# Two more features of one token block by Strassen's seven products, in a fused attention and two-MLP kernel

## The chip, the cores and the metric

The kernel runs on one core of a Trainium2 chip. The metric is the device time of one execution in microseconds (us); before the change it is 573.19 us, the median of three runs (573.0 to 573.52).

## The reference

Attention with 4 sink keys and a window of 128 (2 batches, 8 heads, 768 positions, head size 64) gives 1536 tokens of 512 values. Two MLPs follow, each with 2048 hidden values:

```
keep = is_sink | in_window
a = softmax(where(keep, q @ k.T / 8, -1e9));  x = a @ v        # (1536, 512)
h = x @ w1_in;  g = h * clip(h + 3, 0, 6) / 6;  x = g @ w1_out  # first MLP
h = x @ w2_in;  g = h * sigmoid(1.702 * h);     y = g @ w2_out  # second MLP
```

All inputs, weights included, are given in 64 bits; the kernel converts the weights on the chip. The output is in 32-bit floats.

## The kernel before

The 1536 tokens are three blocks of 512, named by their first token: 0, 512 and 1024. The 2048 hidden values are 16 features of 128. Every operand of a matmul is split into a high and a low part, and every product is made of three matmuls (high x high, high x low, low x high). An ordinary item is one feature of one block: `up` makes four products of 512 columns (12 matmuls, L1143) and a gate, `down` makes four (12 matmuls, L1192).

The first MLP's items are, in this order: block 0 features 0 to 7, block 512 features 0 to 7 and 8 to 15, block 1024 features 0 to 7 (the list `BLOCKS`), then features 8 to 15 of blocks 0 and 1024 together (items of kind "both" and "rest", for the blocks named by `BOTH`). Item 24 is the first of block 1024, items 30 and 31 are its features 6 and 7, item 32 is the first "both".

Both features of a "both" pair are made by Strassen's scheme. The up-projection of two features for the 512 tokens is seen as a product of 2 x 2 blocks, which takes seven block products in place of eight. `weights` combines the weights of the two features (four additions or subtractions of 256 columns on DVE, L610) and splits four operands (casts at L450 and L452, subtractions at L563). `half_pair` makes the seven products, each of 6 matmuls of 256 columns (L723), and puts them together: `put` copies (L740), `add` adds (L747), `clip` makes the gate in two steps (L756, L761). Ordinary items have their gate at L1155 and L1160. The sums of the tokens that Strassen's scheme needs are made by `halve`, once for a block: for each of four slices a copy on the SP queue (L812) and an adding DMA on the POOL queue (L817) into a buffer of the ring "spare", then subtractions (L826), casts (L836) and subtractions for the low parts (L841). Its operand t1 takes the place of half of the block's own columns in `xy`. In the kernel before, `halve` is called for both blocks at the first "both" item.

The order of the work on each engine is found ahead of time by a planner (`Plan.issue`): it puts each operation on an engine and takes, among those that could start within SLACK of the soonest, the one with the earliest due time. Operations that two engines can do go to the one with the smaller end, where PACT and PDVE make ACT and DVE look slower by that share. Due times come from constants: attention tiles from RAMP0, RAMP, PAIR and PAIR2, items from RAMP0, RAMP, START and the rates RATE (the first 8 items) and RATE2 (the next 16), their down-projections DOWN later. A long operation waits up to HOLD for one that is due MARGIN sooner. On the chip each engine runs its own list in that order and waits only for its operands and buffers.

Attention (12 tiles of 128 tokens; scores L1366, transposes L1417, values L1440 and L1448, softmax L1381, L1389, L1398, L1408) and weight conversion (L480, L485, L493, L501, L508 for each feature of each MLP) are mixed with the first MLP's items. The second MLP takes block 512 by ordinary items and blocks 0 and 1024 together by another Strassen scheme (L635, L939). Per MLP product, the names in the rows are: `w0h`, `w0l` the split input weights, `wg` the ring that holds the split output weights and the gates, `sh`, `sl` split combinations, `xt` the split token sums.

Of the kernel before, what the change touches and what calls it, by code (L numbers as in the profile page):

```python
# [33 lines left out]
NVB = 3  # L34
NVC = 3
SLACK = 50
HOLD = 425
MARGIN = 18538
LONG = 1000
ISSUE = 1300  # L40
ADD_DMA = 4500
PACT = 0.1
PDVE = 0.5
STRETCH = 1.0
LATER = 1000000
H_BANKS = 3
RAMP0 = 7993
RAMP = 1510
PAIR = 4538
PAIR2 = 5889  # L50
DOWN = 7000
START = 3000
RATE = 1.61
RATE2 = 1.21
NU = 3
NG = 2
PX = 8
# [3 lines left out]

BLOCKS = [(0, 0, 8), (512, 0, 8), (512, 8, 16), (1024, 0, 8)]
BOTH = (0, 1024)

# [5 lines left out]
def tile_sink_window_attention_moe_moe2(  # L72
# [164 lines left out]
    with tc.tile_pool(name="msk", bufs=1) as mp:  # L237
# [6 lines left out]
        t0 = mp.tile([P, P], F32, name="t0")  # L244
# [270 lines left out]
    def plan_mlps(plan, blocks, item_due, late=None):  # L515
# [27 lines left out]
        def split(i, part):  # L543
            f = items[i][3]
            return split_of(plan.wf[f], slice(512 * part, 512 * (part + 1)), f"w{part}", part, i >= second - NF + 4)
# [24 lines left out]
        def split_g(u, after, act=True):  # L570
            gh, gl = Buf(cls="gh"), Buf(cls="gl")
            plan.op(
                [("ACT", 520)] + ([] if act else [("DVE", 335)]),
                lambda e: copy(e, gh.tile, parted(u.tile)), after, reads=[u], writes=[gh], chain="g",
            )
            plan.op(
                [("DVE", 602)],
                lambda e: e.tensor_tensor(  # L578
                    out=gl.tile, in0=parted(u.tile), in1=gh.tile.bitcast(F32), op=ALU.subtract
                ),  # L580
                after, reads=[u, gh], writes=[gl],
            )
            return gh, gl
# [9 lines left out]
        def weights(i, cls):  # L593

            f1, f2 = items[i][3], items[i][3] + 1
            w1, w2 = plan.wf[f1], plan.wf[f2]
            a11, a12 = (lambda x=x: w1.tile.bitcast(F32)[:, x * 256 : (x + 1) * 256] for x in range(2))
            a21, a22 = (lambda x=x: w2.tile.bitcast(F32)[:, x * 256 : (x + 1) * 256] for x in range(2))
            sa, sb = Buf(cls=cls, kind="m"), Buf(cls=cls, kind="m")
            s1, s4 = (lambda x=x: sa.tile[:, x * 256 : (x + 1) * 256] for x in range(2))  # L600
            s3, s2 = (lambda x=x: sb.tile[:, x * 256 : (x + 1) * 256] for x in range(2))
            for to, x, y, how, reads, into in (
                (s1, a21, a22, ALU.add, [w2], sa),
                (s3, a11, a21, ALU.subtract, [w1, w2], sb),
                (s2, s1, a11, ALU.subtract, [w1, sa], sb),
                (s4, a12, s2, ALU.subtract, [w1, sb], sa),
            ):
                plan.op(
                    [("DVE", 335)],
                    lambda e, to=to, x=x, y=y, how=how: e.tensor_tensor(out=to(), in0=x(), in1=y(), op=how),  # L610
                    None, reads=reads, writes=[into], chain="mix",
                )
            full = slice(0, 512)
            wa, wb = split_of(w1, full, "w0"), split_of(sb, full, "s")
            wc, wd = split_of(sa, full, "w0"), split_of(w2, slice(256, 512), "s")
            return wa, wb, wc, wd
# [62 lines left out]
        def both(i):  # L679

            if i in g:
                return
            if i == second:
                for t0 in BOTH:
                    halve(t0, due[i])
            ws = weights(i, "spare")
            us = half_pair(i, BOTH[0], ws, [Buf(cls="u") for _ in range(2)], due[i])
            for n, u in enumerate(us):
                g[i + n] = split_g(u, due[i] + 6000, False)
            holes = []  # L690
            for n in range(2):
                w = plan.wf[items[i + n][3]]
                holes.append(Buf(wf[items[i + n][3]].bitcast(F32)[:, :512]))
                holes[n].readers = list(w.readers)
            half_pair(i, BOTH[1], ws, holes, due[i] + 7 * 672)
            for n in range(2):
                wo[i + n] = split(i + n, 1)
                kept_u[items[i + n][3]] = holes[n]

        def rest_of(i):  # L700

# [101 lines left out]
        def halve(t0, when):  # L803

            s, first, last = t0 // 512, slice(0, P), slice(P, 256)
            extra[t0, "t1"] = True
            full = [Buf(cls="spare") for _ in range(NC)]
            x = [[b for half in halves(t0, 512) for b in plan.x[half][c]] for c in range(NC)]
            for c in range(NC):
                plan.op(  # L810
                    [("SP", 262144 / RATE_DMA)],
                    lambda e, c=c: e.dma_start(out=parted(full[c].tile), in_=xyl[s][:, :, c, :].bitcast(F32)),  # L812
                    when, reads=x[c], writes=[full[c]], after=plan.done,
                )
                plan.op(
                    [("POOL", ADD_DMA)],
                    lambda e, c=c: e.dma_start(  # L817
                        out=parted(full[c].tile), in_=xyh[s][:, :, c, :].bitcast(F32), accum_op=ALU.add
                    ),
                    when, reads=x[c], writes=[full[c]],  # L820
                )

            def take(a, ac, b, bc, to, tc):
                plan.op(
                    [("DVE", 335)],
                    lambda e: e.tensor_tensor(  # L826
                        out=parted(to.tile)[:, :, tc], in0=parted(a.tile)[:, :, ac], in1=parted(b.tile)[:, :, bc],
                        op=ALU.subtract,
                    ),
                    when, reads=[y for y in (a, b) if y is not to], writes=[to],  # L830
                )

            def parts(src, cols, hi, lo, his, los):
                n = cols.stop - cols.start
                plan.op(
                    [("ACT", 520 if n > P else 300)], lambda e: e.copy(hi(), parted(src.tile)[:, :, cols]), when,  # L836
                    reads=[src], writes=his,
                )
                plan.op(
                    [("DVE", 602 if n > P else 335)],  # L840
                    lambda e: e.tensor_tensor(  # L841
                        out=lo(), in0=parted(src.tile)[:, :, cols], in1=hi().bitcast(F32), op=ALU.subtract
                    ),
                    when, reads=[src] + his, writes=los,
                )

            for j in range(2):
                a, b = full[j], full[2 + j]
                for t in ("t2", "t3", "t4"):
                    extra[t0, t, j] = [Buf(), Buf()]  # L850
                e0 = 6 * BOTH.index(t0) + 3 * j
                at = lambda k, cols, e0=e0: late()["x"](e0 + k)[:, :, cols]
                take(a, last, a, first, a, first)
                take(b, last, a, last, a, last)
                take(b, last, a, first, b, last)
                take(b, first, b, last, b, first)
                both = extra[t0, "t2", j]
                extra[t0, "t4", j] = both
                parts(b, slice(0, 256), lambda at=at: at(0, slice(0, 256)), lambda at=at: at(1, slice(0, 256)), both[:1], both[1:])
                hi, lo = extra[t0, "t3", j]  # L860
                parts(a, last, lambda at=at: at(2, first), lambda at=at: at(2, last), [hi], [lo])
                his, los = ([plan.x[half][j][k] for half in halves(t0, 512)] for k in range(2))
                parts(
                    a, first, lambda j=j: xyh[s][:, :, j, last], lambda j=j: xyl[s][:, :, j, last], his, los,
                )
# [387 lines left out]
        for i in range(len(items)):  # L1253
            f = items[i][3]
            if first_use.get(f) == i:
                plan_convert(plan, f, None)
                if f + nst < NF:
                    plan_load_w(plan, w1, f + nst, None)
                else:
                    plan_load_w(plan, w2, f + nst - NF, None)  # L1260
            {"pair": pair, "both": both, "rest": rest_of}.get(items[i][0], up)(i)
            if i:
                down(i - 1)
            f = items[i][3]
            if i < second + NF and last_use[f] == i:
                plan_convert(plan, f, None)
                if f + nst < NF:
                    plan_load_w(plan, w2, f + nst, None)
# [453 lines left out]
```

## Time and profile before

| | before |
|---|---|
| median of the runs | 573.19 us |
| the profiled execution | 572.57 us |
| its span | 570.8 us |
| PE busy | 555.3 us (97%) |
| DVE busy | 483.1 us (85%) |
| ACT busy | 398.0 us (70%) |
| POOL busy | 64.0 us (11%) |
| chain that ended last, by engine | PE 90%, DVE 4%, DMA 2%, issue 1%, SP queue 1% |

PE is the matmul engine, PEld its weight loads, DVE the vector engine, ACT the scalar engine, POOL and SP the two that issue DMAs here. The chain is followed back from the last instruction: at each step to what released it, or to the instruction before it on its engine.

### The profile page before, as it was taken

How to read it: one execution, taken by the hardware profiler on the slowest of the kernel's cores; microseconds unless marked ns; L12 is line 12 of the kernel's file. 1: busy time of each engine (PE TensorE's matmuls, PEld its weight loads, DVE VectorE, ACT ScalarE, POOL GpSimd, SP SyncE). 2: the span in 40 equal slices, each digit the busy share in tenths (PEclk: the TensorE clock that was granted, in tenths of full speed). 3: DMA queues.
4: the chain of work that ended last, by engine and by line, in shares of the span. 5: the costliest groups of instructions: out<-in, count | busy, mean ns of one | idle time of the engine just before them, and what ended most of it. 6: DMA issues, size and time to landing. Idle time of an engine off the chain costs nothing.

```text
span 570.8 us, 11900 instructions
## 1 busy us (share of the span) xinstructions
PE 555.3 (97%) x4626; PEld 496.0 (87%) x4626; DVE 483.1 (85%) x1045; ACT 398.0 (70%) x849; POOL 64.0 (11%) x70
## 2 busy tenths in 40 slices
PE   6799999999999999999999999999999999999996
PEld 6678888888888888889999888888888888999996
DVE  6899999989999579999999999999567655667784
ACT  6798888854747587577775575765479787768762
POOL 0000000000000212000000000000013334765000
PEclk9989999999999999999999999999999999999998
DMA  8985544143352724212224043223034477999512
GB/s 260 373 253 189 170 145 162 42 140 126 114 170 82 179 79 71 45 66 75 75 75 144 5 148 130 91 88 134 0 93 75 75 108 149 169 183 198 98 38 79
DMA packets 27824, 69.89 MB, mean 122 GB/s; under 512 B 2736, under 2 KB 15024, under 8 KB 23664
## 3 DMA queue, kind: packets, MB, share of 16 engines
q1 hardware_dynamic: 15248, 53.06, 28.0%
q0 software_dynamic: 12224, 15.73, 17.5%
q8 instruction: 38, 0.62, 0.5%
q10 hardware_dynamic: 288, 0.26, 0.2%
q14 instruction: 26, 0.21, 0.1%
HBM read 47.02 MB, written 3.15 MB: 88 GB/s over the span
## 4 chain that ended last, share of the span: by engine, by line
PE 90%; DVE 4%; DMA 2%; issue 1%; SPq 1%; ACT 0%
PE bank L1192 29%; PE bank L1143 21%; PE bank L939 13%; PE bank L635 13%; PE bank L723 7%; PE bank L1417 3%; PE bank L1366 2%; DMA wf<-in_kq_dram 2%; PE bank L1440 1%; PE bank L1448 1%; DVE wf L501 1%; DVE pexp L1381 1%; DVE wf L508 1%; DVE pexp L1408 0%; DVE wf L493 0%
## 5 line engine op out<-in xcount | busy, mean ns | idle before, releaser
L1192 PE MATMUL bank<-wg 128*128 128x512 f32 x768 | 188.5, 381 | 0.3 <-DVE u L1160 0.3
L1192 PEld LDWEIGHTS bank<-wg 128*128 128x128 f32 x768 | 142.0, 189 | 19.6 <-DVE u L1160 0.7
L1143 PE MATMUL bank<-xy,w0h 128*128 128x512 f32 x384 | 116.4, 384 | 1.4 <-ACT xy L450 1.1
L1143 PEld LDWEIGHTS bank<-xy,w0h 128*128 128x128 f32 x384 | 71.1, 189 | 11.9 <-issue 1.3
L450 ACT CAST wg<-wf 128x512 fp32r<-128x512 f32 x83 | 51.1, 618 | 33.6 <-PE bank L1192 24.8
L1143 PE MATMUL bank<-xy,w0l 128*128 128x512 f32 x192 | 72.9, 380 | 0.1
L887 POOL DMA_DIRECT2D wf<-wf x24 | 29.0, 1301 | 228.5 <-ACT wf L868 193.1
L1389 ACT ACTIVATE pexp<-pexp,nb 128x196 f32<-128x196 f32 x96 | 43.1, 452 | 9.1 <-DVE nb L1381 8.9
L563 DVE TENSOR_TENSOR wg<-wf,wg 128x512 fp32r<-128x512 f32 x64 | 44.1, 690 | 5.8 <-ACT wg L450 5.6
L563 DVE TENSOR_TENSOR w0l<-wf,w0h 128x512 fp32r<-128x512 f32 x60 | 41.2, 687 | 3.6 <-ACT w0h L450 3.4
L480 ACT ACTIVATE wf<-stage 128x1024 f32<-128x1024 f32 x32 | 37.8, 1183 | 7.9 <-DMA stage<-in_w_dram 7.9
L1143 PEld LDWEIGHTS bank<-xy,w0l 128*128 128x128 f32 x192 | 36.3, 189 | 5.6 <-DVE w0l L563 0.5
L1155 ACT ACTIVATE u<-bank,three 128x512 f32<-128x512 f32 x32 | 21.8, 681 | 25.4 <-PE bank L1143 25.4
L578 DVE TENSOR_TENSOR wg<-u,wg 128x512 fp32r<-128x512 f32 x56 | 38.3, 689 | 1.3 <-ACT wg L450 1.0
L501 DVE SCALAR_TENSOR_TENSOR wf<-stage,wf 128x1024 int32<-128x1024 int32 x32 | 39.1, 1223 | 0.1
L508 DVE SCALAR_TENSOR_TENSOR wf<-stage,wf 128x1024 int32<-128x1024 int32 x32 | 39.1, 1221 | 0.0
L589 ACT ACTIVATE u<-bank 128x512 f32<-128x512 f32 x32 | 19.1, 596 | 27.4 <-PE bank L1143 20.0
L635 PE MATMUL bank<-xy,w0h 128*128 128x512 f32 x128 | 38.1, 379 | 0.0
L450 ACT CAST wg<-u 128x512 fp32r<-128x512 f32 x47 | 29.0, 621 | 6.8 <-DVE u L1160 4.4
L1381 DVE CUSTOM_DVE_ANT_0 pexp<-bank,mask 128x196 f32<-128x196 f32 x96 | 30.6, 356 | 1.3 <-ACT pexp L1389 0.4
L1417 PE MATMUL bank<-ident,pexp 128*128 128x128 f32 x192 | 28.8, 294 | 2.8 <-DVE pexp L1408 2.6
L1417 PEld LDWEIGHTS bank<-ident,pexp 128*128 128x128 f32 x192 | 24.0, 151 | 6.8 <-issue 2.5
(245 smaller groups left out, 1220.2 us busy)
## 6 DMA issues: line engine op xcount, KB each, us to landing
stage<-in_w_dram SPq DMA_DIRECT2D x32, 1024.0 KB, 4.9
wf<-wf POOLq DMA_DIRECT2D x24, 256.0 KB, 3.8
wf<-in_kq_dram SPq DMA_DIRECT2D x8, 520.0 KB, 11.2
vc<-in_vc_dram SPq DMA_DIRECT2D x12, 320.0 KB, 4.9
vb<-in_v_dram SPq DMA_DIRECT2D x10, 256.0 KB, 6.2
kept<-in_kq_dram SPq DMA_DIRECT2D x4, 520.0 KB, 11.2
vc<-xy SPq DMA_DIRECT2D x7, 256.0 KB, 2.6
vc<-xy POOLq DMA_DIRECT2D x7, 256.0 KB, 4.7
```

Source lines behind the costliest of these rows:

```text
L450: eng.copy(out, in_)
L501: lambda e: e.scalar_tensor_tensor(out=w.tile, in0=top, scalar=-0x40000000, in1=w.tile, op0=ALU.bitwise_and, op1=ALU.bitwise_or),
L508: lambda e: e.scalar_tensor_tensor(out=w.tile, in0=low, scalar=29, in1=w.tile, op0=ALU.logical_shift_right, op1=ALU.bitwise_or),
L563: lambda e: e.tensor_tensor(out=lo.tile[at], in0=of(), in1=hi.tile[at].bitcast(F32), op=ALU.subtract),
L578: lambda e: e.tensor_tensor(out=gl.tile, in0=parted(u.tile), in1=gh.tile.bitcast(F32), op=ALU.subtract),
L635: e.matmul(bank.tile, l, woven(r), start=(begin and j == 0 and k == 0), stop=(j == 1 and k == 2), skip_group_check=True,)
L723: e.matmul(bank.tile[:, :256], l, woven(r), start=(begin and j == 0 and k == 0), stop=(j == 1 and k == 2), skip_group_check=True,)
L939: e.matmul(to, l, woven(t), start=(begin and n == 0 and m == 0 and e4 % share == 0), stop=(n == pairs - 1 and m == 2), skip_group_check=True,)
L1143: e.matmul(h.tile[:, :n], w, woven(x), start=(c == 0 and k == 0), stop=(c == NC - 1 and k == 2))
L1192: e.matmul(yb.tile, l, woven(r), start=(begin and k == 0), stop=(end is not None and k == 2))
L1389: lambda e, n=n: e.activation(pes[n].tile[:, :W], pes[n].tile[:, :W], AF.Exp, bias=nbs[n].tile, scale=-1.0, accum_out=z.tile[:, n : n + 1],),
L1417: e.transpose(pt.tile[:, n * P : (n + 1) * P], pes[2 * a + j].tile[:, x * P : (x + 1) * P], ident)
```

## The change

A constant OWN = 6 is added. The items of block 1024 with feature 6 or more (features 6 and 7, items 30 and 31) are made by a new function `own`: it calls `halve` for block 1024 if that is not done, combines the weights of the pair and calls `half_pair` for block 1024 alone. `both` calls `halve` for each block that has none yet, so for block 0 only. Nine planner constants are changed as well.

```diff
-HOLD = 425
+HOLD = 376
-PDVE = 0.5
+PDVE = 0.71
-RAMP0 = 7993
+RAMP0 = 7638
-PAIR = 4538
-PAIR2 = 5889
-DOWN = 7000
-START = 3000
+PAIR = 4370
+PAIR2 = 5073
+DOWN = 6456
+START = 344
-RATE2 = 1.21
+RATE2 = 1.1
+OWN = 6
...
-            if i == second:
-                for t0 in BOTH:
+            for t0 in BOTH:
+                if (t0, "t1") not in extra:
                     halve(t0, due[i])
...
+        def own(i):
+
+            if i in g:
+                return
+            if (BOTH[1], "t1") not in extra:
+                halve(BOTH[1], due[i])
+            ws = weights(i, "spare")
+            for n, u in enumerate(half_pair(i, BOTH[1], ws, [Buf(cls="u") for _ in range(2)], due[i])):
+                g[i + n] = split_g(u, due[i] + 6000, False)
+                wo[i + n] = split(i + n, 1)
...
-            {"pair": pair, "both": both, "rest": rest_of}.get(items[i][0], up)(i)
+            alone = late and items[i][0] == 1 and items[i][1] == BOTH[1] and items[i][3] >= OWN
+            {"pair": pair, "both": both, "rest": rest_of, 1: own if alone else up}.get(items[i][0], up)(i)
```

## Rows read from the trace of the kernel before

**Rows 1.** Busy time by stretch: stretch, length, each engine's busy us (instructions), clock, DMA.
```profile
20.00:40.00 20.00, 16.45 (x410) 14.11 (x410) 17.27 (x64) 16.95 (x54) 0.00 (x0) 0.91 0.98 335
40.00:60.00 20.00, 18.17 (x230) 15.31 (x226) 19.93 (x54) 16.72 (x42) 0.00 (x0) 1.00 0.60 183
60.00:560.00 500.00, 500.00 (x3614) 447.71 (x3612) 426.79 (x835) 349.65 (x705) 62.58 (x60) 1.00 0.42 106
```

**Rows 2.** Chain of waits, whole span: start us, length us, what.
```profile
5.44 12.08 DMA wf<-in_kq_dram
...
24.32 2.92 issue
...
58.54 4.80 PE bank L1192 x21
...
490.60 75.05 PE bank L939 x672
```

**Rows 3.** Chain of waits from 32.6 to 58.5 us, shares by line.
```profile
by line: DVE wf L501 13.1%; DVE pexp L1381 12.5%; DVE wf L508 12.1%; DVE pexp L1408 8.4%; DVE wf L493 7.1%; DVE wf L485 7.0%; DVE u L1160 7.0%; issue 5.2%; DVE wg L578 5.0%; DVE w0l L563 4.8%; DVE xy L1467 4.7%; DVE wg L563 4.7%; DVE z L139
```

**Rows 4.** Chain of waits, runs of matmuls of 512 (L1192) and 256 columns (L723).
```profile
329.33 7.77 PE bank L1192 x36
...
265.77 2.68 PE bank L723 x24
...
257.52 4.98 PE bank L723 x42
```

**Rows 5.** Groups by line and shape: count | busy us, mean ns | idle before, releaser.
```profile
L563 DVE TENSOR_TENSOR w0l<-wf,w0h 128x512 fp32r<-128x512 f32 x60 | 41.2, 687 | 3.6 <-ACT w0h L450 3.4
...
L723 PEld LDWEIGHTS bank<-xy,w0h 128*128 128x128 f32 x128 | 20.3, 191 | 0.9 <-ACT vb L740 0.2
...
L1160 DVE SCALAR_TENSOR_TENSOR u<-u,bank 128x512 f32<-128x512 f32 x32 | 21.8, 683 | 6.7 <-ACT u L1155 6.6
...
L610 DVE TENSOR_TENSOR aside<-wf 128x256 f32<-128x256 f32 x16 | 6.7, 422 | 0.0
...
L756 ACT ACTIVATE u<-bank,three 128x256 f32<-128x256 f32 x12 | 5.4, 473 | 2.9 <-PE bank L723 1.6 <-DVE bank L747 1.4
...
L761 DVE SCALAR_TENSOR_TENSOR u<-u,bank 128x256 f32<-128x256 f32 x12 | 4.8, 418 | 0.5 <-ACT u L756 0.4
```

**Rows 6.** Busy time by stretch, from 180 to 400 us.
```profile
180.00:220.00 40.00, 40.00 (x357) 34.52 (x356) 29.66 (x66) 27.33 (x58) 8.77 (x7) 1.00 0.54 119
220.00:400.00 180.00, 180.00 (x995) 162.04 (x994) 177.02 (x310) 117.77 (x220) 1.22 (x1) 1.00 0.25 86
```

**Rows 7.** Timeline near 400 us: start us, length us, instruction, idle before.
```profile
400.44 1.24 DVE L508 SCALAR_TENSOR_TENSOR wf<-stage,wf 128x1024 int32<-128x1024 int32 x1
...
403.67 0.69 DVE L563 TENSOR_TENSOR w0l<-wf,w0h 128x512 fp32r<-128x512 f32 x1 [1.38 <-ACT w0h L450]
...
408.16 0.59 PE L1143 MATMUL bank<-xy,w0h 128*128 128x512 f32 x2
```

**Rows 8.** DMA issues of `halve`: count, KB each, us from issue to landing.
```profile
vc<-xy SPq DMA_DIRECT2D x7, 256.0 KB, 2.6
vc<-xy POOLq DMA_DIRECT2D x7, 256.0 KB, 4.7
```

**Rows 9.** Groups by line and shape, the adding DMAs of `halve`.
```profile
L817 POOL DMA_DIRECT2D vc<-xy x7 | 9.1, 1528 | 29.3 <-PE bank L1192 16.0 <-DVE xt L841 12.9 <-PE bank L1143 0.4
```

**Rows 10.** Timeline near 240 us: last operand of `halve` in xt, item 30's up-projection.
```profile
239.45 0.69 DVE L841 TENSOR_TENSOR xt<-vc,xt 128x512 fp32r<-128x512 f32 x1 [0.35 <-ACT xt L836]
...
241.73 0.59 PE L1143 MATMUL bank<-xy,w0h 128*128 128x512 f32 x2
```

**Rows 11.** Chain of waits, six matmuls elsewhere and six behind attention scores.
```profile
76.30 1.29 PE bank L1143 x6
...
85.58 1.49 PE bank L1192 x6
```

**Rows 12.** Timeline near 43 us: the first up-projection.
```profile
42.61 0.45 PE L1143 MATMUL bank<-xy,w0h 128*128 128x512 f32 x1 [1.15 <-ACT xy L450]
```

## The prediction

> **What bounds the kernel now.** I read the share of each engine by stretch first [rows 1]. From 60 to 560 us TensorE (PE) is busy in every microsecond, at the full granted clock. Before that it is idle for 20.00 - 16.45 = 3.55 us of the stretch 20 to 40 and 1.83 us of 40 to 60, with the clock at 0.91 of full in the first of these. A busy PE need not be a PE at its peak, so the chain of waits comes next [rows 2]: at 58.54 us it arrives on PE, its last stretch there is the 672 matmuls of L939 that start at 490.60, and between the two all its pieces are matmuls (a few hundred, listed as alternating L1143, L1192, L635, L723 and attention). So the time is: when PE gets full (58.5 us), plus the matmuls still to do, plus a tail that this change does not touch. Before 58.5 us the chain runs through VectorE (DVE) [rows 3]: from 32.6 on it is weight conversion (L485, L493, L501, L508, together 39.3% of 25.9 us), softmax (L1381, L1408), splits and gates, all on DVE. Two things can move the time: fewer or cheaper matmuls, and a PE that is full sooner.
>
> **The product, on PE.** Features 6 and 7 of block 1024 were two ordinary items: 2 x 4 x 3 = 24 matmuls of 512 columns for the up-projection. They become one `half_pair`: seven products of 6 matmuls of 256 columns, 42 in all. The down-projection (L1192) stays. 36 matmuls of 512 columns take 7.77 us, 215.8 ns each; 24 of 256 columns take 2.68 us, 111.7 ns each [rows 4]. Removed 24 x 215.8 = 5.18 us, added 42 x 111.7 = 4.69 us: 0.49 us less. Low end: one full half pair took 4.98 us [rows 4], which leaves 0.20 us. All of it lies on the path, as PE has no idle time there. I take 0.49, since 24 in a row is the undisturbed figure.
> [...]
>
> **What it adds on DVE and ScalarE (ACT).** The weights of the pair are combined by 4 subtractions and additions of 256 columns, and four operands are split instead of two (three of 512 columns, one of 256). The results take 3 additions and 4 clips of 256 columns where two clips of 512 did before. In DVE durations [rows 5]: 4 x 0.422 + (0.687 + 0.422) + (3 x 0.422 + 4 x 0.418 - 2 x 0.683) = 1.69 + 1.11 + 1.57 = 4.37 us. On ACT it is at most 7 x 0.473 = 3.3 us of results [rows 5] and two casts, against 62 us idle on ACT from 220 to 400 [rows 6]; I cost that at nothing.
> DVE is the place to look: 177.02 of 180 us busy from 220 to 400 [rows 6], so 4.37 us more finds only 2.98 us of idle. The rest makes later what DVE does last before it gets slack at 402 us. The last conversion (L508) ends at 401.68, its split (w0l) at 404.36, and the matmuls that read it start at 408.16 [rows 7]: 3.8 us of lead behind the split, which itself waits 1.38 us for ACT and not for DVE. Cover is 2.98 + 3.8 + 1.38 = 8.2 us, against 4.37 plus the 0.49 by which PE comes sooner. So I cost DVE's work at nothing. If the idle pieces can't be used and only the 3.8 us are left, PE stalls 4.37 + 0.49 - 3.8 = 1.1 us.
>
> **What it moves.** `halve(1024)` now belongs to item 30 instead of item 32, ahead of `halve(0)`. It issues 4 copies on SP, 4 adding DMAs on POOL, 8 DVE subtractions, 6 casts on ACT and 6 subtractions for the low parts. No instruction is new. On SP the copies of block 1024 wait for the last attention tile, and the weight loads stand behind them; on POOL nothing else is queued until far later. The chain for one quarter is 2.6 us (SP) + 4.7 us (POOL) [rows 8], then two subtractions, a cast and another subtraction, some 2 us. The previous last operand of either block was written at 239.45 + 0.69 = 240.1 us, because one adding DMA had waited 12.9 us for a buffer [rows 9, 10]; item 30 starts on PE at 241.73 [rows 10]. Were nothing reordered, the operands would be there 1.6 us ahead of the first of them that is used (the third product, 1.3 us later still). With 1024 first, the margin grows: nothing. A new wait is the overwriting of block 1024's own columns (operand t1): its cast on ACT must wait until item 29's up-projection has read them, and the casts of the next weights queue behind it. But t1 is the fifth product, 4 x 6 x 0.112 = 2.7 us after the pair begins; nothing again.
>
> **The due times.** They set only the order on each engine. From the constants, item 0 is due at 32.14 instead of 35.15 us, the first four attention tiles 0.36 us sooner, item 30 12.1 us sooner and the last tile 17.9 us sooner. From 60 us on PE is full in either order, so there the order matters only through the changes between kinds of matmul. Six 512-column matmuls behind attention scores take 1.49 us, elsewhere 1.29 [rows 11]: 0.2 us for each return. Four more or fewer such returns are 0.8 us either way; I take zero.
> The ramp is where order matters. The first up-projection starts at 42.61 after 1.15 us of waiting for the cast of the fourth tile [rows 12]; in front of it stands a DVE that never rests. The gain ends at PE's idle 3.55 + 1.83 = 5.38 us [rows 1]. The loss ends at one feature's conversion put ahead of the fourth tile: three of them make 39.3% of 25.9 us [rows 3], 3.4 us each. PDVE 0.71 for 0.5 is the one constant with a sign: a scale or a cast that could go to either engine now goes to ACT more readily. The scales on DVE (L1408) are 8.4% of 25.9 us = 2.2 us of the chain [rows 3]. A quarter of them, 0.5 us, is my estimate; where DVE already has a queue the choice fell on ACT before, so most will not flip.
>
> **Sum.** 0.49 + 0.5 = 1.0 us less. The profiled execution took 572.57 us (span 570.8 and 1.77 around it), so 571.6; the median of the three runs lies 0.62 above the profiled one: 572.2 us. What a measurement of this kernel can tell from no change is about 0.2%, 1.15 us; the forecast falls just inside it.
>
> **Rivals.**
> (a) The ramp gets much shorter: PE loses half of its idle there, 2.7 us, and one stall fewer of the kind of the 2.92 us "issue" piece [rows 2] would lift the clock as well. For it: the whole chain before 58.5 us is order on DVE. Against it: the first 17.5 us hang on DMA [rows 2], and the issue stall is not set by due times. With the 0.49: 573.19 - 3.2 = 570.0; from 570 to 571.4.
> (b) PE's saving is paid back by DVE: a stall of 1.1 us near 400 us cancels 0.49 and the ramp's 0.5; 573.3, no difference. For it: 2.98 us of idle in 180. Against it: the leads above, and 10.3 us of idle on DVE from 180 to 220 [rows 6] that earlier attention could use.
> (c) The other side: the ramp gets longer. Item 0 comes due 2.66 us sooner against the first four tiles, so a conversion passes the fourth tile's work on DVE, and PE's first up-projection waits for it. It decides once a conversion that ended behind that tile's L1467 ends ahead of it. Price 3.4 us at most, two thirds of it typical: 573.19 - 0.49 + 2.3 = 575.0. For it: the 1.15 us wait is on that tile already. Against it: the first conversion has long been done by then.
> (d) The pair alone finds its operands late: POOL's adds wait for buffers as one did for 12.9 us. PE would stall 2.3 us or so (about the lead of 1.6 us turned round): 574.5. Against it: the earlier attention.
> (e) The weight loads bind after all: 42 loads of 0.191 us are 8.0 us in place of 5.18; 573.19 + 2.8 = 576.0. Against it: the spacing of 111.7 ns. [...]
>
> **Chances.** Forecast 0.45 (its own range 571.4 to 573.0; a little under half of it lies below the bound of faster), (a) 0.23, (b) 0.12, (c) 0.14, (d) 0.05, (e) 0.01. Faster: 0.20 + 0.23 = 0.43. Slower: 0.14 + 0.05 + 0.01 and 0.02 of (b) = 0.22. The same: 0.35. The range from 570.2 to 574.6 leaves out half of (a) and the far ends of (c) and (e).
>
> **What would show it.** In the profile after: L1143 with 552 matmuls in place of 576 and L723 with 378 in place of 336, at 112 ns apart; PE without idle from some 58 us to the end. If the forecast holds, the chain reaches PE for good between 57 and 59 us and the stretch from there to the last matmul is about 0.5 us shorter. Under (a) it gets there at 56 or before, under (c) at 60 or later. Under (b) a wait of L1143 for w0l (DVE) appears between 330 and 410 us; under (d) one of L723 for xt or xy near 235 us. I am wrong in the main if PE's stretch is not shorter, that is if the returns between kinds outweigh 0.5 us, or if the ramp moves by over 1.5 us.

## The result, and the profile after

The changed kernel takes 580.2 us (median of four runs, 578.09 to 580.34), the kernel before 573.13 us beside it: a ratio of 1.0113, 95% interval [1.0099, 1.0128]. The forecast was 572.2 us; the change makes the kernel 1.1% slower. Its profiled execution took 580.33 us with a span of 578.5 us, 7.7 us more than before.

First the share of busy time by stretch of the kernel after (columns as in [rows 1]: PE, weight loads, DVE, ACT, POOL, then clock and DMA share):

```profile
20.00:40.00 20.00, 16.38 (x386) 14.88 (x380) 14.91 (x59) 14.63 (x48) 0.00 (x0) 0.82 0.82 309
40.00:60.00 20.00, 17.86 (x212) 15.11 (x208) 18.60 (x47) 16.63 (x41) 0.00 (x0) 0.91 0.53 154
60.00:560.00 500.00, 498.39 (x3637) 443.80 (x3634) 426.88 (x842) 351.90 (x716) 62.42 (x60) 1.00 0.42 108
```

Against [rows 1], three things differ. From 20 to 40 us DVE is busy for 14.91 us instead of 17.27; PE seems as busy as before, but at a clock of 0.82 instead of 0.91, and with 24 matmuls fewer. From 40 to 60 us DVE lacks another 1.33 us and the clock is 0.91. And from 60 to 560 us, where PE was never idle, it is idle for 1.61 us.

To put these on one scale, I add up from the matmul records what the matmuls done until a moment would take undisturbed (512 columns 215.8 ns, 256 columns 111.7 ns, [rows 4]; the attention's matmuls at their closest spacing) and take it from the time gone by. The difference to the same sum of the kernel before is called the excess here; it is good to about 0.2 us late in the span, and to about half a us at 60 us, where it hangs on the spacing that is taken for the attention's matmuls. For the kernel after it is 4.2 us at 60 us, 4.8 at 120, 4.5 at 220, 6.0 at 240, 7.0 at 320, 7.8 at 360 and 8.0 at the end. Take off the 0.49 us that the pair saves, and 7.5 of the span's 7.7 us are found: a little over half in the ramp (the stretch before PE is full), most of the rest in small stalls between 220 and 360 us. Another 0.3 us lie behind the last matmul.

The chain of waits of the kernel after, in the ramp (start us, length us, what); the pieces left out between 28.31 and 31.50 are the same tile's L1453 and L1461:

```profile
23.28 1.44 PE bank L1379 x87
24.72 3.08 issue
27.81 0.51 PE bank L1379 x9
28.31 0.62 PE bank L1453 x4
...
31.50 0.45 PE bank L1461 x8
31.99 0.46 issue
32.45 1.50 ACT pexp L1419 x4
33.96 1.77 ACT pexp L1402 x8
36.14 0.25 DVE pexp L1394
36.39 0.93 DVE pexp L1421 x4
```

Here the chain runs on PE up to 32 us; [rows 3] had it on DVE from there on. Behind the stall of 3.08 us (2.92 before, [rows 2]) stand 9 scores and then all 48 matmuls of the second tile's values; the transposes come only then, at 31.86 us. In the kernel before, the timeline of PE (start us, length us, instruction, idle before) has another order behind the same stall:

```profile
23.93 0.38 PE L1440 MATMUL bank<-pts,vb 128*64 128x128 f32 x3
27.23 0.32 PE L1440 MATMUL bank<-pts,vb 128*64 128x128 f32 x1 [2.92 <-issue]
27.24 0.55 PE L1448 MATMUL bank<-pts,vc 68*64 68x64 f32 x8
27.72 0.93 PE L1366 MATMUL bank<-wf 64*64 64x64 f32 x48
28.59 1.97 PE L1417 MATMUL bank<-ident,pexp 128*128 128x128 f32 x8
```

There the values were nearly done when the stall came, 48 scores took 0.93 us, and the transposes began at 28.59. Transposes are what DVE waits for: they free the buffers of `pexp` (8 in the ring, one tile's worth) into which its next softmax goes. The timeline of DVE in the kernel after shows the hole:

```profile
27.63 1.19 DVE L509 SCALAR_TENSOR_TENSOR wf<-stage,wf 128x1024 int32<-128x1024 int32 x1
32.58 0.36 DVE L1394 CUSTOM_DVE_ANT_0 pexp<-bank,mask 128x196 f32<-128x196 f32 x1 [3.76 <-PE bank L1430]
```

Not all of the 3.76 us are additional. In the kernel before, DVE waits from 24 to 46 us too, 2.4 us in all, mostly for ACT's cast of a tile's values (waited for, us in total, times, longest):

```profile
DVE xy L1467 <- ACT xy L450: 1.8, 1, 1.8
```

From 20 to 40 us DVE is busy 2.36 us less than before, as the table of stretches shows. The first up-projection starts at 46.28 us instead of 42.61 [rows 12], and until then DVE has been busy as long in the kernel after (34.90 us) as in the one before (35.05): it was not given more work, it stood still longer.

Behind that start the clock adds to it. From 47.07 us the chain of waits is on PE, and the clock is then at half of full (PEclk 0.50). The chain, the row by stretch, and the timeline of DVE, all of the kernel after:

```profile
47.07 6.27 PE bank L1155 x20
47.60:50.90 3.30, 3.30 (x9) 2.60 (x8) 3.19 (x10) 2.20 (x5) 0.00 (x0) 0.50 0.66 145
52.15 0.69 DVE L1172 SCALAR_TENSOR_TENSOR u<-u,bank 128x512 f32<-128x512 f32 x1 [1.33 <-ACT u L1167]
```

Some eight spacings of matmuls of 512 columns take 3.30 us there, against 1.7 at 215.8 ns each, and DVE waits 1.33 us for the gate behind them: the 1.33 us that it lacks from 40 to 60 us. By this estimate some 1.6 of the 4.2 us come from this stretch of clock. The values behind the stall run at half clock as well (PEclk 0.50 from 28 to 32 us): their 48 matmuls take 3.6 us of the chain, against 2.0 us at the full clock in the kernel before (51.1 to 53.1 us), so the clock has a part in DVE's hole, too. The rest is the order.

The pair itself came out as worked out. Two pieces of the chain of waits after, to set beside [rows 4]:

```profile
271.48 2.68 PE bank L735 x24
...
327.34 7.77 PE bank L1204 x36
```

Both are equal to before to the last digit; L1155 has 552 matmuls, L735 has 378. But PE now waits, where the list of waits of PE between 60 and 560 us was empty before (waited for, us in total, times, longest):

```profile
PE bank L1155 <- DVE w0l L564: 0.8, 1, 0.8
PE bank L1204 <- DVE wg L579: 0.3, 1, 0.3
PE bank L735 <- ACT vb L752: 0.2, 1, 0.2
```

The first two stand behind `halve` in DVE's list, which now belongs to item 30. The timeline of the kernel after, DVE and PE:

```profile
216.72 0.43 DVE L838 TENSOR_TENSOR vb<-vb 128x256 f32<-128x256 f32 x1 [1.10 <-DMA vb<-xy]
219.16 0.43 DVE L838 TENSOR_TENSOR vc<-vc 128x256 f32<-128x256 f32 x1 [1.41 <-DMA vc<-xy]
...
223.64 0.68 DVE L564 TENSOR_TENSOR w0l<-wf,w0h 128x512 fp32r<-128x512 f32 x1
...
224.38 0.48 PE L1155 MATMUL bank<-xy,w0l 128*128 128x512 f32 x1 [0.79 <-DVE w0l L564]
226.92 1.35 PE L1204 MATMUL bank<-wg 128*128 128x512 f32 x5 [0.33 <-DVE wg L579]
```

DVE stands 1.10 and 1.41 us at subtractions of `halve` whose adding DMA has not landed; all that is queued behind them moves back, and two operands that PE needs, a split w0l and a wg, come late. That `halve` is the cause is read from this order; no run moved it alone.

### The profile page after: what moved, and what is told of

It reads as the page before. It is cut to its first block, busy times and chain, and to the rows that moved or that the text cites. A ratio compares the mean times of both kernels' runs of the same rounds, so it can differ in the third digit from the quotient of the medians.

```text
span 578.5 us, 11960 instructions
## 1 busy us (share of the span) xinstructions
PE 561.0 (97%) x4644; PEld 500.8 (87%) x4644; DVE 484.2 (84%) x1049; ACT 402.9 (70%) x863; POOL 63.8 (11%) x70
## 4 chain that ended last, share of the span: by engine, by line
PE 85%; DVE 9%; ACT 2%; issue 2%; DMA 1%; DVEq 0%; ACTq 0%
PE bank L1204 26%; PE bank L1155 19%; PE bank L951 13%; PE bank L636 13%; PE bank L735 4%; PE bank L1430 3%; PE bank L1379 3%; PE bank L1453 2%; PE bank L1461 2%; ACT pexp L1402 1%; DVE wg L564 1%; DMA vc<-xy 1%; DVE wg L579 1%; DVE wf L509 1%; DVE w0l L564 1%
## 5 line engine op out<-in xcount | busy, mean ns | idle before, releaser
L1204 PE MATMUL bank<-wg 128*128 128x512 f32 x768 | 190.8, 382 | 0.6 <-DVE wg L579 0.3
L1155 PE MATMUL bank<-xy,w0h 128*128 128x512 f32 x368 | 112.8, 388 | 1.7 <-issue 1.4
L1155 PEld LDWEIGHTS bank<-xy,w0h 128*128 128x128 f32 x368 | 68.9, 191 | 11.9 <-issue 1.5
L1155 PE MATMUL bank<-xy,w0l 128*128 128x512 f32 x184 | 70.5, 383 | 0.8 <-DVE w0l L564 0.8
L1155 PEld LDWEIGHTS bank<-xy,w0l 128*128 128x128 f32 x184 | 35.2, 191 | 6.2 <-DVE w0l L564 1.2
L636 PE MATMUL bank<-xy,w0h 128*128 128x512 f32 x128 | 38.1, 379 | 0.0
L1167 ACT ACTIVATE u<-bank,three 128x512 f32<-128x512 f32 x30 | 20.5, 685 | 18.9 <-PE bank L1155 18.5
L451 ACT CAST w0h<-wf 128x512 fp32r<-128x512 f32 x48 | 29.6, 618 | 1.1 <-PE bank L636 0.5
L451 ACT CAST wg<-u 128x512 fp32r<-128x512 f32 x45 | 27.6, 620 | 2.9 <-DVE u L1172 1.4
## 6 DMA issues: line engine op xcount, KB each, us to landing
kept<-in_kq_dram SPq DMA_DIRECT2D x4, 520.0 KB, 10.2
```

Source lines behind the costliest of these rows:

```text
L451: eng.copy(out, in_)
L636: e.matmul(bank.tile, l, woven(r), start=(begin and j == 0 and k == 0), stop=(j == 1 and k == 2), skip_group_check=True,)
L1155: e.matmul(h.tile[:, :n], w, woven(x), start=(c == 0 and k == 0), stop=(c == NC - 1 and k == 2))
L1204: e.matmul(yb.tile, l, woven(r), start=(begin and k == 0), stop=(end is not None and k == 2))
```

## The experiments

Times are medians beside runs of the kernel before on the same chip (573.09 us for the first four, 573.41 for the next four, 573.19 for e9 to e11, 573.68 for e12). The excess is that of the one profiled execution. In e5 and e6 the padding counts as work done. A theory's number in one expectation is not that of another.

| run | us | ratio to before, 95% | excess at 60 us | at the end |
|---|---|---|---|---|
| after | 580.2 | 1.0113 [1.0099, 1.0128] | 4.2 | 8.0 |
| e1 pair, old constants | 576.21 | 1.0054 [1.0033, 1.0075] | 0.7 | 4.3 |
| e2 constants, no pair | 578.67 | 1.0083 [1.0058, 1.0109] | 4.7 | 6.9 |
| e3 before, START | 577.37 | 1.0071 [1.0048, 1.0094] | 3.9 | 6.3 |
| e4 before, PDVE | 578.87 | 1.0095 [1.0064, 1.0126] | 5.6 | 7.3 |
| e5 before, padded | 577.45 | 1.0062 [1.0038, 1.0085] | 1.9 | 3.5 |
| e6 after, padded | 585.0 | 1.0192 [1.0167, 1.0218] | 5.2 | 8.9 |
| e7 as e1, less work on DVE | 577.05 | 1.005 [1.0031, 1.0068] | 1.1 | 4.5 |
| e8 before, less work on DVE | 572.93 | 0.9984 [0.9968, 1.0] | 0.7 | 0.7 |
| e9 after, old ramp | 576.14 | 1.0047 [1.0028, 1.0066] | 0.0 | 4.2 |
| e10 after, transposes first | 577.71 | 1.0076 [1.0051, 1.0101] | 1.5 | 6.1 |
| e11 as e1, combinations later | 575.26 | 1.0037 [1.0025, 1.0049] | 0.0 | 3.3 |
| e12 as e1, combinations apart | 574.78 | 1.0016 [1.0001, 1.003] | 0.9 | 2.9 |

**The two halves of the change, and two constants alone.** e1 is the kernel after with the nine constants of before; e2 the kernel after with OWN = 16, so that no pair is made alone; e3 and e4 change one constant of the kernel before.

```diff
-OWN = 6
+OWN = 16        # e2
-START = 3000
+START = 344     # e3
-PDVE = 0.5
+PDVE = 0.71     # e4
```

e1: 

> The pair made alone by seven products (OWN = 6), with all planner constants of the kernel before. Theory 1 (two causes: the new order of the first 60 us costs some 4.2 us, the pair's work on DVE and its late operands some 3.7 us, less the 0.5 us of matmuls saved): the ramp is that of before, so 573.1 + 3.7 - 0.5 = 576.3, with stalls of PE behind DVE between 215 and 350 us. Rival (all of the loss is due to the new due times, the pair costs nothing): 572.6. Rival (all is due to the pair): 580.

e2: 

> The nine new constants, with features 6 and 7 of block 1024 made by ordinary items as before. Theory 1: the ramp's loss of some 4.2 us stays and the loss after 215 us goes: 577.3. Rival (all due to the due times): 580. Rival (all due to the pair): 573.

e3: 

> The kernel before with START = 344 alone, which brings every MLP item and the later attention tiles 2.66 us nearer to the first four tiles. Theory 1a (START is what spoils the ramp: conversions pass the attention tiles on DVE): some 3 to 4 us longer, 576 to 577, all of it lost before 60 us. Theory 1b (PDVE does it, by moving work to ACT): 573.

e4: 

> The kernel before with PDVE = 0.71 alone. Theory 1a (START spoils the ramp): 573, or 0.5 less as predicted for scales that go to ACT. Theory 1b (PDVE spoils it): 576 to 577, lost before 60 us, with the exponentials on ACT on the chain.

Both halves cost. The pair alone has a ramp like before's and loses 3.6 us after 220 us; the constants alone have the ramp's loss and some 2 us behind it. Alone they cost 3.1 and 5.6 us, together 7.1, not 8.7: what is lost late hangs on the whole order. START alone and PDVE alone each bring a loss in the ramp (3.9 and 5.6 us at 60 us). Part of it may be clock: the profiles of e2, e3 and e4 have the same stretch at half clock as that of the kernel after, 3.4 us long, from 46.6 to 47.6 us on. The profiled run of e3, at a mean clock of 0.984, took 578.98 us, its four others, at 0.988 to 0.991, 577.17 to 577.57. All of e2, e3 and e4 have 9 scores and the 48 matmuls of the second tile's values behind the stall, ahead of the third tile's transposes. DVE waits for that once: for the transposes 4.1 us in e2 and 4.6 in e3 (0.2 before), in e4 4.6 us for ACT's copy of the values themselves, which its list has first there.

**Padding PE's instructions.** To move the stall at 24 us against the order, tiny matmuls were put ahead of the first transposes, 22 in the kernel before (e5) and 50 in the kernel after (e6); nothing else is changed.

```diff
+                    if d == 0 and a == 0:
+                        for _ in range(22):
+                            e.matmul(pt.tile[:4, :4], ident[:, :4], ident[:, :4], start=True, stop=True)
```

e5: 

> The kernel before with 22 tiny matmuls (4 x 4 results, overwritten right after) put ahead of the first transposes, where PE waits for the softmax anyway. In all six traces PE stands still for some 3 us behind its 473rd matmul, whatever the order; the 44 more of the records should move that point 44 matmuls earlier in the program, ahead of the second tile's values and the last scores instead of behind most of the values. Theory 2 (where this stall falls decides what the softmax engines have to do meanwhile): DVE and ACT run dry for 3 to 4 us near 28 us, the chain reaches PE for good some 2 to 4 us later, 575 to 577. Rival (the order on DVE and ACT decides, the stall's place is of no account): 573 to 573.5.

e6: 

> The kernel after with 50 such tiny matmuls, so that the stall falls ahead of two blocks of scores and eight transposes and not ahead of the last scores and 48 matmuls of values. Theory 2: the scores come right behind the stall, DVE is fed sooner, 1 to 3 us of the ramp come back: 577 to 579. Rival (the place is of no account): 580 or, with the additional matmuls on the path, 581.

The padding disturbed what it was to test. The waits of PE in e5 from 8 to 60 us show the stall of 3.1 us still there (it begins at 25 us, and stands 22 matmuls earlier in the program, not 44) and another of 3.7 us in front of it, at 9.8 us, in the first transposes:

```profile
PE bank L1417 <- issue: 3.7, 1, 3.7
PE bank L1366 <- issue: 3.1, 1, 3.1
```

e6 has the new stall too, and more later. Both runs are inconclusive for the ramp; they are of use for where such stalls stand (last section).

**Less work on DVE.** In e7 (as e1) and e8 (before) the first step of each second-MLP conversion, the clamp, leaves out all but 8 of 1024 columns; the order stays.

```diff
+        n = 8 if f in plan.made_once else 1024
+        plan.made_once.add(f)
-                out=w.tile.bitcast(F32), in0=w.tile.bitcast(F32), scalar1=TOP_LO, scalar2=TOP_HI,
+                out=w.tile.bitcast(F32)[:, :n], in0=w.tile.bitcast(F32)[:, :n], scalar1=TOP_LO, scalar2=TOP_HI,
```

e7: 

> The pair with the old due times, and in the conversion of the second MLP's weights the clamp (a DVE operation of 0.69 us) is cut from 1024 to 8 columns for all 16 features; the other columns are left as they are. The order on every engine is that of the run with the pair alone; DVE has some 9 us less to do after 230 us. Theory 3 (PE's stalls in the run with the pair alone, 3.7 us between 240 and 400 us, are DVE being full): most of them go, 573 to 573.6. Rival (they come from the order, a queue that waits for another engine, not from how much DVE does): 575.5 to 576.2.

e8: 

> Control: the kernel before with the same 16 clamps cut from 1024 to 8 columns. In the kernel before PE never waits for DVE after 58.5 us, so both theories expect 573 to 573.4; less than that would mean that DVE's load costs PE something there too.

DVE's busy time falls from 485.8 us in e1 to 479.5 in e7, and the time does not fall at all. The control e8 is 0.16% faster than the kernel before, at the edge of its interval. PE's waits from 205 to 425 us in e7 are those of e1 (its lines are three further down):

```profile
PE bank L1158 <- DVE w0l L567: 1.2, 1, 1.2
PE bank L738 <- ACT u L755: 0.4, 1, 0.4
PE bank L1207 <- DVE wg L582: 0.3, 1, 0.3
```

So the late loss is not a DVE that has too much to do. What it is, the timeline of e1 shows, DVE and then PE:

```profile
378.12 1.30 DVE L1135 SCALAR_TENSOR_TENSOR xt<-vc,xt 128x512 fp32r<-128x512 f32 x2
...
379.32 0.70 DVE L1135 SCALAR_TENSOR_TENSOR xt<-vb,xt 128x512 fp32r<-128x512 f32 x1
...
379.92 0.69 DVE L1135 SCALAR_TENSOR_TENSOR xt<-vc,xt 128x512 fp32r<-128x512 f32 x1
...
380.52 1.30 DVE L1135 SCALAR_TENSOR_TENSOR xt<-aside,xt 128x512 fp32r<-128x512 f32 x2
...
381.73 0.70 DVE L564 TENSOR_TENSOR w0l<-wf,w0h 128x512 fp32r<-128x512 f32 x1
...
382.48 0.48 PE L1155 MATMUL bank<-xy,w0l 128*128 128x512 f32 x1 [1.30 <-DVE w0l L564]
```

Six operations that make operands for the second MLP, not used before 418 us, stand ahead of the split that PE needs now; w0h, from which the split is made, was there at 380.5 us.

**The old ramp in the kernel after** (e9), and **the transposes put first** (e10, one order added on PE and nothing else):

```diff
-PDVE = 0.71
+PDVE = 0.5      # e9, with RAMP0 = 7993 and START = 3000
+        valued[1].order.append(turns[9])   # e10: values of tile 1 behind two turns of tile 2
```

e9: 

> The kernel after with only START, PDVE and RAMP0 set back (3000, 0.5, 7993); the pair and the other six constants stay new. Theory 1 (the ramp's order is what costs: behind the stall at 24 us the values of the second tile come ahead of the third tile's transposes): the order on PE is again that of the kernel before up to the first up-projection, so the excess at 60 us falls from 4.2 to 0.7 us or less, the first up-projection starts at 42.6 to 43.2 us and not at 46.3; what is left is late stalls of the kind of the run with the pair alone, 1.5 to 4 us: 574.5 to 577. Rival (the pair itself costs, in whatever order): 579 to 581, with the ramp short and the loss all behind 200 us. Third case (the new later constants were searched for a late part that fits the new ramp, so the late part gets worse): over 577.

e10: 

> The kernel after; one order is added: on PE the values of the second tile come behind the first 8 transposes of the third tile, not ahead of them. Nothing is added or left out. Theory 1 (VectorE starves behind the stall at 24 us because the values, 3.4 us at half clock, stand ahead of the transposes that free the ring pexp): the first transposes behind the stall start at 28.2 to 29 us and not at 31.9, VectorE's wait of 3.8 us on them falls under 1 us, the excess at 60 us falls from 4.2 to between 0.5 and 2.5 us, and the time to 576.5 to 579. Rival (VectorE has other work that could have been done there, or what is won is waited for again at the values, which now come later, by the split of the tile): excess at 60 us 3.5 to 4.5, time 579.5 to 581.

e9 has the ramp of before back to the last 0.1 us, and the first up-projection at 42.45 us. By stretch it reads as [rows 1]:

```profile
20.00:40.00 20.00, 16.52 (x412) 14.23 (x412) 17.28 (x63) 17.10 (x55) 0.00 (x0) 0.91 0.98 335
40.00:60.00 20.00, 18.16 (x224) 15.23 (x221) 19.93 (x54) 16.50 (x42) 0.00 (x0) 1.00 0.62 186
```

Its late loss of 4.2 us is even larger than e1's, with other waits (1.0 us for a split wg at 343 us, 0.8 for ACT's L752 at 262 us). In e10 the timeline has the transposes right behind the 9 scores, and DVE goes on 3.2 us sooner than in the kernel after:

```profile
28.23 0.51 PE L1379 MATMUL bank<-wf 64*64 64x64 f32 x9 [3.36 <-issue]
28.66 1.97 PE L1430 MATMUL bank<-ident,pexp 128*128 128x128 f32 x8
...
29.39 0.36 DVE L1394 CUSTOM_DVE_ANT_0 pexp<-bank,mask 128x196 f32<-128x196 f32 x1 [1.83 <-PE bank L1430]
```

2.7 of the 4.2 us come back in its profile, although it has a stall of 1.6 us more, at 20 us. But e10 differs in the clock too: it has none of the stretch at half clock near 48 us, and its row for the same 3.30 us reads:

```profile
47.60:50.90 3.30, 3.30 (x19) 2.90 (x18) 3.27 (x9) 3.12 (x9) 0.00 (x0) 1.00 0.51 106
```

Its first up-projection starts at 44.96 us, 1.3 us sooner than in the kernel after; by the matmuls done, about as much of the 2.7 us (1.6) is won between 47.5 and 51 us, at the higher clock. No run holds the clock and changes the order alone. DVE's wait halves, where under 1 us was expected: it runs out of work at 27.5 us, and the stall on PE lasts to 28.2. Its nine runs spread from 575.09 to 580.38 us, and its interval just touches that of the kernel after. So e9 shows that three of the nine constants bring the whole of the ramp's loss, and e10 that the place of the transposes makes about half of DVE's hole; how the 4.2 us divide between order and clock stays an estimate.

**The second MLP's combinations later** (e11, e12): e1 with one due time changed.

```diff
-                    mixes(when + 40000)
+                    mixes(when + 46000)   # e11; 60000 in e12
```

e11: 

> The run with the pair alone (old constants), with the due time of the second MLP's combinations of tokens 46 us behind the output of block 512 instead of 40 us. By that the split w0l stands ahead of the six operations that scale them (3.7 us in a row on VectorE). Theory 2 (the late loss with the pair is the order in VectorE's queue): the wait of 1.30 us of the up-projection for w0l at 382 us goes, 574.3 to 575.5 instead of 576.2, and the excess between 380 and 400 falls from 1.7 to under 0.5 us. Rival (VectorE has no slack there, and the loss moves to the next split or to the combined tokens): 576 to 577, with a wait of 1 us or more of a matmul somewhere between 380 and 420 us.

e12: 

> The run with the pair alone (old constants), with the due time of the second MLP's combinations of tokens 60 us behind the output of block 512 instead of 40 us, so that on VectorE the six operations that scale them stand apart, with conversions and splits between them, and not in a row. Theory 2 (what is lost late is the order in VectorE's queue): neither the stall of 1.46 us at 382 us of the run with the pair alone nor the one of 0.99 us at 389 us of the run with 46 us comes, the excess over before between 380 and 400 us is under 0.4 us, and the time is 574.0 to 574.9. Rival (VectorE has no slack left there, so whoever is last is late): a stall of 0.8 us or more of a matmul for a split, a gate or a combination between 380 and 425 us, and 575.2 to 576.5.

In e11 the stall at 382 us is gone, and one for another split has come at 389 us, behind the same six operations, which still stand in a row. PE's waits from 205 to 425 us in e11:

```profile
PE bank L1204 <- DVE wg L564: 0.8, 1, 0.8
PE bank L735 <- ACT u L752: 0.4, 1, 0.4
PE bank L1204 <- DVE wg L579: 0.3, 1, 0.3
```

In e12 they stand apart, and nothing waits near 380 us any more:

```profile
PE bank L735 <- ACT u L752: 0.4, 1, 0.4
PE bank L1204 <- DVE wg L579: 0.2, 1, 0.2
```

The excess between 380 and 400 us goes from 1.7 us (e1) over 1.1 (e11) to 0.2 (e12), and the time from 576.21 over 575.26 to 574.78. DVE had room for all of it. Most of what is left of e12 to before is 0.9 us in the ramp and four gaps of 0.2 to 0.6 us at 230, 252, 336 and 337 us, which e1 and e11 have as well. No version here beats the kernel before; one without those gaps would win 0.49 us, less than a measurement of this kernel can tell from no change, and was not searched for.

## Why the prediction was wrong

**The product on PE: right.** 24 matmuls of 512 columns left and 42 of 256 came, at the same 215.8 and 111.7 ns. The rival of binding weight loads is out: in the kernel after a load of L735 takes 191 ns, yet its matmuls follow each other after 111.7 ns.

**The due times: the step that failed.** I took 0.5 us of gain, on the ground that PDVE is "the one constant with a sign": more scales and casts on ACT, so less on a DVE that never rests. Measured: a loss of 4.2 us at 60 us, and PDVE alone costs 5.6 there (e4). DVE does rest in the ramp, as [rows 1] says: 17.27 of 20.00 us from 20 to 40. And no scale moved: up to the first up-projection DVE makes 24 of them and ACT 8 in both kernels; what went to ACT are two copies of `pts` (L452 before), 1.38 us of DVE. The sum priced DVE's work; what decided was when PE and ACT hand DVE what it waits for, the buffers of `pexp` above all. I had the stall of 2.92 us in [rows 2] and said rightly that due times don't set it, but did not look at what stands right behind it on PE, and who waits for that. Each reshuffle that was run (START, PDVE, or all nine constants) put the second tile's values ahead of the third tile's transposes. The clock was no term of the sum at all: up to 60 us it is at half of full for 17.1 us, in three stretches, against 6.8 us before. Time at half clock is not lost by itself: e11 has 10.2 us of it, all before 22 us, and an excess of 0.0. The third stretch, with PE on the chain, costs some 1.6 us by the estimate above, and the one run of the kernel after with a mean clock of 0.995 took 578.09 us, those at 0.984 to 0.986 took 580.1 to 580.3.

**Rival (c), a longer ramp, had the sign** (chance 0.14) and not the mechanism: I had a conversion pass the fourth tile's work on DVE, at 3.4 us at most. DVE was busy as long as before until the first up-projection; it had nothing that it could do. The price was above that bound. Rival (a) counted on one stall fewer: in e8 and e11 the stall behind matmul 473 lasts 0.8 and 1.0 us instead of 2.92, with an excess of 0.7 and 0.0 us at 60 us. Nothing was won by it. That one stall fewer lifts the clock as well was my estimate from the trace of before, where the clock is at half of full from 28.53 to 31.94 us, behind the stall's end at 27.23. The runs are divided on it: e11, with the short stall, has no half clock behind 22 us, but 10.2 us of it ahead; and in e6 the clock is 1.00 from 20 to 40 us, though PE is busy for only 1.67 of the 4.00 us from 24 to 28.

**DVE's additional work at nothing: right in amount, wrong in kind.** I held 4.37 us against 8.2 us of cover. DVE's busy time rose by 2.7 us in e1, and e7 shows that taking 6 us away changes nothing. But an engine that works off its list in order is late for one operation while it has room in the mean: 3.6 us were lost with the pair alone. For the largest wait, at 382 us, e11 and e12 show why: something that PE needs soon stood behind something that could wait. For the four smaller gaps (some 1.6 us) that is not shown. That wait is the sign that I gave for rival (b), and its 1.30 us are near the 1.1 us of my bound; but it came from the order and not from the amount. That PE waits for nothing late in the kernel before holds for that very order.

**`halve` at nothing: wrong.** I asked what is behind it on SP and POOL and whether its operands come in time; they do. Behind its subtractions on DVE, which wait for the adding DMAs, stood the splits of the running items: two waits of 1.10 and 1.41 us on DVE, 0.8 and 0.3 on PE, and 1.5 us of excess from 220 to 240 us. What is queued behind a waiting instruction had to be named on DVE as well.

**The sum by measured terms** (profiled executions): +4.2 ramp, +0.3 to 220 us, +1.5 at `halve`, +2.0 in later gaps, -0.5 for the pair: 7.5 us, and with 0.3 behind the last matmul 7.8, for the 7.7 of the spans.

## What to carry to other kernels

Where in-order lists are planned ahead, a new plan is priced by what stands behind each wait and stall that the trace already has, on every engine: a mean share of idle time is no cover for a single operation that comes late. A change whose prize is 0.5 us in 573 should be tried with the old order kept wherever it can be; here the plan's reshuffle cost some 15 times the prize. And where a loss stays though the work on the accused engine is cut (e7), try its order: here that mended the largest stall (e12).

## What the runs showed of the hardware

PE does not wait for operands and buffers alone: it also stands still for nothing that its operands explain ("issue") at fixed places in its own list of instructions. In 13 of the 14 traces a stall of 0.8 to 3.4 us stands behind matmul 473, whether that is a value or a score (e6 has it behind 475); e10 has another behind 347, e6 behind 601 and 726, the padded ones behind 221. The distances are 125 to 127 matmuls; from 347 to 473 the trace of the kernel before has 128 weight loads beside the 126 matmuls, that of the kernel after 126. In the DMA view of the kernel after from 15 to 35 us the queue that it calls "instruction" (packets, MB, share of the 16 engines' time) moves three packets of 16 KB beside data that takes 94%:

```profile
q1 hardware_dynamic: 1885, 6.76, 94.0%
q8 instruction: 3, 0.05, 1.1%
```

The packets and the stalls come together: at these places, in all 14 traces, PE goes on 1.2 to 1.6 us after the end of a packet of this queue, whenever it came to stand (behind 473 in the kernel before at 27.23 us, the packet's end at 25.91; in the kernel after at 27.81 and 26.35). So the stall is short where PE arrives late: 2.9 us from 24.32 us on in the kernel before, 0.8 us from 26.45 us on in e8.

The stall behind 473 falls where the DMA engines are busy for 0.98 of the stretch from 20 to 40 us in the kernel before [rows 1] and 0.82 in the one after. The longest lasts 4.2 us (e6, behind 221), while at other such places none shows (in the kernel before near 600 and 726). From 60 us on, at a DMA share of 0.42, no such stall of over 1 us shows. That these packets wait behind those of the weights is an estimate from these rows; no run here took the traffic away.
